# Attention backward in one kernel: TensorE sums Z and X before it transposes E, ScalarE copies E alone, and VectorE's sums move between its two products

## The chip, the cores and the metric

One Trainium2 chip, one of its cores. The metric is the time of one execution on the device in microseconds. A core has engines that run side by side, each through its own queue in order: TensorE (PE in the profile, PEld its weight loads), VectorE (DVE), ScalarE (ACT), GpSimd (POOL) and the queue that issues most DMAs (SP). They wait for each other on semaphores. SBUF is the working memory, PSUM the memory that TensorE writes to, in banks of 512 f32 a partition.

## What is computed

The reference is the forward pass and all gradients of a gated block: `out = x + attention(xn) * silu(mlp(xn))`, with `xn` a layer norm of x. Cut to the part that matters here:

```python
B, S, D, H = 1, 2048, 512, 32          # Dh = 16
qkv = (x @ wqkv) ...                   # q, k, v: 32 heads of 16
scores = einsum("bhqd,bhkd->bhqk", q, k) * Dh ** -0.5
p = softmax(scores)
o = einsum("bhqk,bhkd->bhqd", p, v)
s = o... @ wo
...
_out, _vjp = jax.vjp(_f, A_x, A_wqkv, A_wo, B_w1, B_b1, B_w2, B_b2)
_grads = _vjp(grad_out)
```

Attention and its backward pass are most of the time: for each head the 2048 x 2048 scores, their exponentials E, the products of E with the gradient of p (called G below), and sums of both over keys (for o and the gradient of q) and over queries (for the gradients of k and v).

## The kernel before

`Pre` computes the projections and the MLP's forward part; `attention_core` does attention, forward and backward together; `Grads` the rest. The change is in `attention_core` alone.

**Blocks and steps.** Heads go in 16 pairs, queries in 4 chunks of 512: 64 blocks. A block goes through 16 key tiles of 128; one tile is a step, so there are 1024 steps `g`, and 20 more at the end. The place of a step in its block is `g % 16`, 0 to 15 below. The loop at the end of `attention_core` emits one step after the other, and on each engine the instructions run in the order in which they are emitted (the order is written by hand; no scheduler moves them).

**A step on TensorE.** Before the change its order is:

- `emit_d`, `emit_s` (L1115, L1093): two matmuls d (the gradient of p, for the two heads) and two matmuls s (the scores of the *next* step), each from 32 rows of the array to 128 columns, 512 wide, so that all four run side by side.
- `emit_T(g - 1)` (L1177): seven transposes of 128 x 128 of E into one PSUM tile tT (the eighth slice of E goes by DMA).
- `emit_XT` (L1233), at place 2 alone: four f32 transposes of the sums X of the block before, into a tile XT of the pool that d uses.
- `emit_x(g - 1, ...)` (L1207, L1210, L1214): three groups of four matmuls of 128 rows to 32 (or 17) columns that add E and G into X; the third group ("g") reads the products gts of the step before.
- `emit_z(g - 20)` (L1291): four matmuls of 128 rows to 32 columns that add transposed G or E of a block 20 steps back into Z. Eight steps make one sum.

**ScalarE.** `emit_exp(g + 1)` (L1102) writes E of the next step (ets) from s; `emit_cT(g - 1)` (L1189) copies the transposed slices from tT to ek in SBUF.

**VectorE.** `emit_mult` (L1132) makes the two products gts = d x E of the two heads. Between them it copies the last `VCOPY[(g - 1) % 16]` of the seven slices of tT (0, 1 or 2 of them; ten in sixteen steps), and ScalarE's copy of the rest waits for it. Behind the products: `emit_xs` (L1223, at place 0) copies a finished X out; `emit_fin` (L1245, L1255, at place 2) copies XT to xt and makes the reciprocal rL, from which GpSimd makes the weights W1 and W2 that Z uses; `emit_acc` (L1303, L1305, at places 3 and 11) adds a finished Z to acc.

**Buffers that make engines wait.** s, tT, X and Z have one PSUM tile each: the next s waits for exp, the next transposes for the copies, the next X for xs, the next Z for acc. d and XT share three tiles: a d waits for the product that read its tile (at place 4 the first d waits for xt, the second for the first product of place 3). xs and xt share one SBUF tile.

**DMAs.** SP issues a transposing DMA of two steps' gts to gk behind every second step's products (L1148), and one or two of slices of E (ekd). GpSimd loads the next pair's operands, each load behind a small copy `tick` that waits for a product.

Of the kernel before, what the change touches and what calls it, by code (L numbers as in the profile page):

```python
# [9 lines left out]
f32 = mybir.dt.float32  # L10
# [43 lines left out]
def op_load_list(k, t, p, ld):  # L54

    L = []
    for hj in range(2):
        h = 2 * p + hj
        L.append(lambda h=h, hj=hj: ld(out=t["KVT"][32 * hj + 1:32 * hj + 17, :], in_=k.KT_s[h * 16:h * 16 + 16, :]))
        L.append(lambda h=h, hj=hj: ld(out=t["QDT"][32 * hj + 1:32 * hj + 17, :], in_=k.QT_s[h * 16:h * 16 + 16, :]))  # L60
        L.append(lambda h=h, hj=hj: ld(out=t["QDT"][32 * hj:32 * hj + 1, :], in_=k.UT_s[h:h + 1, :]))
    for hj in range(2):
        h = 2 * p + hj
        L.append(lambda h=h, hj=hj: ld(out=t["KVT"][64 + 32 * hj:80 + 32 * hj, :], in_=k.VT_s[h * 16:h * 16 + 16, :]))
        L.append(lambda h=h, hj=hj: ld(out=t["QDT"][64 + 32 * hj:80 + 32 * hj, :], in_=k.DOT_s[h * 16:h * 16 + 16, :]))
    L.append(lambda: ld(out=t["NAT"][:].rearrange("q k j c -> q k (j c)"), in_=k.NAT_s[p]))
    return L


def natq_loads(k, t, p, ld):  # L70
    return [lambda n=n, d=d: ld(out=t[n][:].rearrange("q k j c -> q k (j c)"), in_=d[p])
            for n, d in (("NATQq", k.NATQq_s), ("NATQd", k.NATQd_s))]
# [956 lines left out]
def attention_core(ctx, ctx_r, tc, k, grads, Oall, dQall, dKVT_out, ident_f32, ident_bf, npairs=16, nqc=4):  # L1029
    nc = tc.nc  # L1030
# [36 lines left out]
    st_s, st_d, st_et, st_gt, st_T = {}, {}, {}, {}, {}  # L1067
    blk = [dict(Gk={}, Ek={}) for _ in range(NB)]
    cur = {}

    def a_unit(g):
        return (g // 16, g % 16) if 0 <= g < NSTEP else None

    def z_unit(g):
        j = g // 16
        m = g % 8
        return (j, (g % 16) // 8, m % 4, m // 4) if 0 <= j < NB else None
# [38 lines left out]
                         start=True, stop=True, tile_position=(r, 0))  # L1116


    VCOPY = (0, 0, 0, 0, 1, 1, 1, 2, 1, 2, 0, 0, 1, 1, 1, 0)

    def emit_mult(g):
        a = a_unit(g)
        if a is None:
            emit_cT(g - 1, 7 - VCOPY[(g - 1) % 16], 7, nc.vector.tensor_copy)
            return
        kb = a[1]
        if kb % 2 == 0:
            cur["gts"] = gtp.tile([128, 2, 2, 512], bf16, name="gts")
        gts = cur["gts"]
        st_gt[g] = gts  # L1130
        for hj in range(2):
            nc.vector.tensor_tensor(out=gts[:, kb % 2, hj, :].rearrange("k (b q) -> k b q", b=4),  # L1132
                                    in0=st_d.pop((g, hj))[:].rearrange("k (b q) -> k b q", b=4),
                                    in1=st_et[g][:, :, hj, kb % 4, :], op=ALU.mult)
            if hj == 0:
                emit_cT(g - 1, 7 - VCOPY[(g - 1) % 16], 7, nc.vector.tensor_copy)

    def emit_dmat(g):
        a = a_unit(g)
# [28 lines left out]
    def emit_T(g):  # L1168
        a = a_unit(g)
        if a is None:  # L1170
            return
        kk = a[1] % 4
        et = st_et[g]
        t = ps_t.tile([128, 7, 128], bf16, name="tT")
        for i in range(7):
            b = i + a[1] // 4 % 2
            nc.tensor.transpose(t[:, i, :], et[:, b // 2, b % 2, kk, :], ident_bf[:])  # L1177
        st_T[g] = t
        if kk == 0:
            cur["ek"] = ekc.tile([128, 4, 7, 128], bf16, name="ek")  # L1180
            blk[a[0]]["Ek"][a[1] // 4] = cur["ek"]

    def emit_cT(g, lo, hi, copy):

        a = a_unit(g)
        if a is None or lo == hi:
            return
        j, kb = a
        copy(out=blk[j]["Ek"][kb // 4][:, kb % 4, lo:hi].rearrange("q i k -> q (i k)").bitcast(f32),  # L1189
             in_=st_T[g][:, lo:hi].rearrange("q i k -> q (i k)").bitcast(f32))  # L1190

    def emit_x(g, part):
        a = a_unit(g)
# [23 lines left out]
    def emit_xs(g):  # L1217
        a = a_unit(g)
        if a is None or a[1] != 15:
            return  # L1220
        j = a[0]
        xs = xsp.tile([128, 512], f32, name="xs", tag="xs")
        nc.vector.tensor_copy(out=xs[:], in_=blk[j].pop("X")[:])  # L1223
        blk[j]["xs"] = xs

    def emit_XT(g):
        j = g // 16 - 1
        if g % 16 != FIN_AT or not 0 <= j < NB:
            return
        xs = blk[j].pop("xs")  # L1230
        XT = ps_d.tile([128, 4, 128], f32, name="XT", tag="d")
        for qb in range(4):
            nc.tensor.transpose(XT[:, qb, :], xs[:, qb * 128:(qb + 1) * 128], ident_f32[:])  # L1233
        blk[j]["XT"] = XT
# [38 lines left out]
    def emit_z(g):  # L1273
        u = z_unit(g)
        if u is None:
            return
        j, kp, qb, part = u
        if part == 0 and qb == 0:
            blk[j]["Z"] = ps_z.tile([128, 512], f32, name="Z", tag="z")
        Z = blk[j]["Z"]  # L1280
        for par in range(2):
            kc = 2 * kp + par
            for hj in range(2):
                r = 64 * par + 32 * hj
                if part == 0:
                    mv = blk[j]["Gk"][kc][:, :, hj, qb, :]
                elif 2 * qb + hj == 7 * (1 - par):
                    mv = blk[j]["Ek"][(kc, 3)]
                else:
                    mv = blk[j]["Ek"][kc][:, :, 2 * qb + hj - par, :]  # L1290
                nc.tensor.matmul(Z[r:r + 32, :], lhsT=WT[j % 2][1 - part][:, qb, hj, :], rhs=mv,  # L1291
                                 start=(part == 0 and qb == 0), stop=(part == 1 and qb == 3), tile_position=(0, r))

    def emit_acc(g):
        u = z_unit(g)
        if u is None or u[2] != 3 or u[3] != 1:
            return
        j, kp = u[0], u[1]
        p, qc = blocks[j]
        Z = blk[j]["Z"]  # L1300
        av = acc[:, kp, :]
        if qc == 0:
            nc.vector.tensor_copy(out=av, in_=Z[:])  # L1303
        else:
            nc.vector.tensor_tensor(out=av, in0=Z[:], in1=av, op=ALU.add)  # L1305
        if qc == nqc - 1:
            ob = (outp.tile([128, 512], bf16, name="ob") if kp == 0 or j < NB - 1 else
                  xsp.tile([128, 512], bf16, name="ob", tag="xs"))
            nc.gpsimd.tensor_copy(out=ob[:], in_=av)
            dv = dKVT_out[p * 64:(p + 1) * 64, :].rearrange("r (a b s) -> r a b s", a=2, b=2)  # L1310
            for b in range(2):
                nc.gpsimd.dma_start(out=dv[:, kp, b, :], in_=ob[b * 64:(b + 1) * 64, :])

    FIN_AT = 2
    ZOFF = -20
# [4 lines left out]
    for g in range(NSTEP - ZOFF):  # L1320
        cur["g"] = g
        a = a_unit(g)
        if a is not None:
            j, kb = a
            p, qc = blocks[j]
            if kb == 0 and qc == 0:
                L = natq_loads(k, k.op0, p, nc.gpsimd.dma_start) if p > 0 else []
                if p + 1 < npairs:
                    L += op_load_list(k, OP[(p + 1) % 2], p + 1, nc.gpsimd.dma_start)
                else:  # L1330
                    L += grads.tail_loads(nc.gpsimd.dma_start)
                for i, f in enumerate(L):
                    late.append((g + 16 * (i // 4) + 6 + 3 * (i % 4), f))
        emit_d(g, 0)
        emit_s(g + 1, 0)
        emit_s(g + 1, 1)
        emit_d(g, 1)
        emit_exp(g + 1)
        emit_T(g - 1)
        emit_XT(g)  # L1340
        emit_x(g - 1, "e")
        emit_x(g - 1, "l")
        emit_x(g - 1, "g")
        emit_z(g + ZOFF)
        emit_mult(g)
        emit_xs(g - 1)
        emit_fin(g)
        for it in [x for x in late if x[0] <= g]:
            late.remove(it)

            nc.gpsimd.tensor_copy(out=tick[:], in_=st_gt[g][0:1, kb % 2, 1, 510:512])  # L1351
            it[1]()
        emit_acc(g + ZOFF)
        if g >= NSTEP:
            grads.tail_mid(g - NSTEP)
        emit_cT(g - 1, 0, 7 - VCOPY[(g - 1) % 16], nc.scalar.copy)
        st_T.pop(g - 1, None)
        emit_dmat(g)
        st_gt.pop(g - 2, None)
        st_et.pop(g - 12, None)  # L1360
        if g == NSTEP:
            ctx_r.close()
            grads.tail_open(ps_t, ps_s, ps_d)
# [113 lines left out]
```

## Time and profile before

| | us |
|---|---|
| median of the runs (3) | 2214.51 |
| lowest and highest of them | 2211.53, 2218.92 |
| the profiled execution | 2212.67 |
| its span | 2210.8 |
| attention's part of the span | 221 to 1867 |

Busy in the span: TensorE 2154.0, VectorE 1911.7, ScalarE 1734.2, GpSimd 590.4. The granted clock of TensorE is 0.997 of full speed. In the chain of work that ended last TensorE has 89%, its transposes (L1177) 24%, d 15%, X 20% in three lines, Z 10%.

How long a step of each place takes, from the start of its first d to that of the next step's, by the trace's order of time (medians over the blocks, ns):

| place | 0 | 1 | 2 | 3 | 4 | 5 | 6 | 7 | 8 | 9 | 10 | 11 | 12 | 13 | 14 | 15 |
|---|---|---|---|---|---|---|---|---|---|---|---|---|---|---|---|---|
| ns | 1562 | 1628 | 1993 | 1482 | 1670 | 1563 | 1547 | 1568 | 1554 | 1535 | 1591 | 1532 | 1635 | 1563 | 1548 | 1563 |

A line in the order of time has the start in us from the span's start, the time taken, the engine, the line, the operation and what it writes and reads, "x4" where four alike are merged, and in brackets how long the engine sat idle before and what ended that. Ends of matmuls are modelled, and their waits show best as distances between starts. A line of a group has "busy us, mean ns of one | idle before".

### The profile page before, as it was taken

What the parts mean: (1) busy time and instruction counts of PE and PEld (TensorE: products, weight loads), DVE (VectorE), ACT (ScalarE), POOL (GpSimd) and SP (SyncE); (2) the same over time, 40 slices, a digit from 0 to 9 for tenths busy, and PEclk for the clock granted to TensorE, in tenths of its full rate; (3) what the DMA queues carried; (4) which work ended last, traced back from release to release, by engine and by line L of the source; (5) the groups of instructions that cost most, each with busy time, mean ns of one, the idle gap of its engine ahead of it and who ended that gap; (6) DMA issues with size and microseconds to landing.
All of it is one profiled execution on the core that took longest, in us unless ns stands there. A gap on an engine that the chain in (4) does not pass through costs nothing.

```text
span 2210.8 us, 74213 instructions
## 1 busy us (share of the span) xinstructions
PE 2154.0 (97%) x30690; PEld 1203.2 (54%) x30690; DVE 1911.7 (86%) x3638; ACT 1734.2 (78%) x2481; POOL 590.4 (27%) x1373
## 2 busy tenths in 40 slices
PE   6999999999999999999999999999999999999998
PEld 3444555555555555555555555555555555444444
DVE  6677899999999999999999999999999998797624
ACT  4664888888888888888888888888888887784214
POOL 4375213221222222221322122222222132510002
PEclk9999999999999999999999999999999999999999
DMA  7786999999999999999999999999999999999974
GB/s 232 244 277 200 200 199 192 202 198 194 204 205 195 204 196 197 201 197 202 200 196 203 199 195 198 206 194 204 197 197 206 197 210 211 300 259 235 244 200 156
DMA packets 1422066, 461.14 MB, mean 209 GB/s; under 512 B 1334622, under 2 KB 1405918, under 8 KB 1421728
## 3 DMA queue, kind: packets, MB, share of 16 engines
q1 hardware_dynamic: 1407424, 425.46, 101.4%
q0 software_dynamic: 12720, 29.37, 5.0%
q8 instruction: 240, 3.93, 0.8%
q10 hardware_dynamic: 1584, 1.57, 0.2%
q14 instruction: 98, 0.80, 0.1%
HBM read 62.79 MB, written 64.75 MB: 58 GB/s over the span
## 4 chain that ended last, share of the span: by engine, by line
PE 89%; DVE 4%; ACT 2%; issue 2%; DMA 2%; POOL 1%; SPq 1%; ACTq 0%; DVEq 0%; POOLq 0%
PE tT L1177 24%; PE d L1115 15%; PE X L1207 10%; PE Z L1291 10%; PE X L1210 5%; PE X L1214 5%; PE s L1093 3%; PE ps_dw L742 2%; PE ps_dy L912 2%; PE ps_h L352 2%; PE ps_dw L984 2%; PE ps_m L367 2%; PE ps_dh L878 2%; PE XT L1233 1%; PE ps_qkv L210 1%
## 5 line engine op out<-in xcount | busy, mean ns | idle before, releaser
L1132 DVE TENSOR_TENSOR gts<-d,ets 128x512 bf16<-128x512 f32 x2048 | 1361.6, 683 | 99.4 <-ACT ek L1189 20.5
L1102 ACT ACTIVATE ets<-s 128x1024 bf16<-128x1024 f32 x1024 | 1047.7, 1023 | 198.6 <-PE s L1093 95.5
L1177 PE MATMUL tT<-ident_bf,ets 128*128 128x128 bf16 x7168 | 568.1, 219 | 11.7 <-ACT ek L1189 1.7
L1177 PEld LDWEIGHTS <-ets 128*128 128x128 bf16 x7168 | 444.6, 97 | 237.6 <-issue 235.5
L1189 ACT COPY ek<-tT 128x448 f32<-128x448 f32 (+2 forms) x1024 | 502.2, 490 | 2.8 <-DVE ek L1189 2.1
L1115 PE MATMUL d<-QDT,KVT 32*128 32x512 bf16 x2048 | 459.1, 385 | 0.0
L1093 PE MATMUL s<-QDT,KVT 32*128 32x512 bf16 x2048 | 401.3, 380 | 3.7 <-ACT ets L1102 3.6
L1115 PEld LDWEIGHTS <-KVT 32*128 32x128 bf16 x2048 | 145.6, 91 | 323.3 <-issue 323.3
L1207 PE MATMUL X<-ets,NAT 128*32 128x256 bf16 x4096 | 300.4, 284 | 0.3 <-DVE xs L1223 0.3
L1210 PE MATMUL X<-ets,Lc 128*32 128x256 bf16 x4096 | 289.5, 273 | 0.0
L1214 PE MATMUL X<-gts,NAT 128*17 128x256 bf16 x4096 | 289.5, 273 | 0.0
L1351 POOL COPY tick<-gts 1x2 bf16<-1x2 bf16 x205 | 35.7, 174 | 612.3 <-DVE gts L1132 612.3
L1291 PE MATMUL Z<-gk,W 128*32 128x512 bf16 x2048 | 197.9, 379 | 1.0 <-DVE acc L1305 1.0
L1291 PE MATMUL Z<-ek,W 128*32 128x512 bf16 x1792 | 198.4, 379 | 0.0
L1207 PEld LDWEIGHTS <-NAT 128*32 128x32 bf16 x4096 | 106.0, 93 | 110.8 <-issue 11.3
L1256 POOL TENSOR_TENSOR W<-NATQq,rL 128x128 bf16<-128x128 bf16 x64 | 25.4, 396 | 526.1 <-DVE rL L1255 438.4
L1093 PEld LDWEIGHTS <-KVT 32*128 32x128 bf16 x2048 | 139.2, 91 | 12.8 <-issue 9.6
L1189 DVE COPY ek<-tT 128x64 f32<-128x64 f32 (+1 forms) x576 | 131.6, 229 | 0.7
L1291 PEld LDWEIGHTS <-W 128*32 128x32 bf16 x4096 | 109.8, 97 | 11.5 <-issue 1.5
L1210 PEld LDWEIGHTS <-Lc 128*32 128x32 bf16 x4096 | 107.8, 96 | 0.0
L1214 PEld LDWEIGHTS <-NAT 128*17 128x17 bf16 x4096 | 103.4, 92 | 3.0
L1291 PE MATMUL Z<-ekd,W 128*32 128x512 bf16 x256 | 97.0, 379 | 0.0
(246 smaller groups left out, 2318.7 us busy)
## 6 DMA issues: line engine op xcount, KB each, us to landing
gk<-gts SPq DMA_TRANSPOSE x512, 5.3
H1T_s<-h1r SPq DMA_DIRECT2D x28, 256.0 KB, 4.1
HGT_s<-hgT SPq DMA_DIRECT2D x8, 896.0 KB, 4.5
DH_s<-stg SPq DMA_DIRECT2D x12, 512.0 KB, 3.2
hch<-DH_s SPq DMA_DIRECT2D x12, 512.0 KB, 4.4
gp<-H1T_s SPq DMA_DIRECT2D x9, 512.0 KB, 7.6
out_dram<-ob_w POOLq DMA_DIRECT2D x36, 128.0 KB, 4.2
NAT_s<-NS SPq DMA_DIRECT2D x4, 1056.0 KB, 6.1
```

Source lines behind the costliest of these rows:

```text
L352: nc.tensor.matmul(ps[:], lhsT=w1_sb[:, ic, fc * 128:(fc + 1) * 128], rhs=yT[:, ic, g * 512:(g + 1) * 512], start=(ic == 0), stop=(ic == I ...
L367: nc.tensor.matmul(ps[:], lhsT=hgT[:, g % 2, fc, t4 * 128:(t4 + 1) * 128], rhs=w2_sb[:, fc, :], start=(fc == 0), stop=(fc == FC - 1))
L1093: nc.tensor.matmul(s[:, hj, :], lhsT=op["KVT"][r:r + 32, kb * 128:(kb + 1) * 128], rhs=op["QDT"][r:r + 32, qc * 512:(qc + 1) * 512], start ...
L1102: nc.scalar.activation(out=st_et[g][:, :, :, a[1] % 4, :].rearrange("k b h q -> k h b q"), in_=cur["s"][:].rearrange("k h (b q) -> k h b q ...
L1115: nc.tensor.matmul(d[:], lhsT=op["KVT"][r:r + 32, kb * 128:(kb + 1) * 128], rhs=op["QDT"][r:r + 32, qc * 512:(qc + 1) * 512], start=True, ...
L1132: nc.vector.tensor_tensor(out=gts[:, kb % 2, hj, :].rearrange("k (b q) -> k b q", b=4), in0=st_d.pop((g, hj))[:].rearrange("k (b q) -> k b ...
L1177: nc.tensor.transpose(t[:, i, :], et[:, b // 2, b % 2, kk, :], ident_bf[:])
L1189: copy(out=blk[j]["Ek"][kb // 4][:, kb % 4, lo:hi].rearrange("q i k -> q (i k)").bitcast(f32), in_=st_T[g][:, lo:hi].rearrange("q i k -> q ...
L1207: nc.tensor.matmul(X[r:r + 32, 0:256], lhsT=NATt[:, kb, hj, 1:33], rhs=ev, start=(kb == 0), stop=False, skip_group_check=True, tile_positi ...
L1210: nc.tensor.matmul(X[r:r + 32, 256:512], lhsT=Lc[:], rhs=ev, start=False, stop=False, skip_group_check=True, tile_position=(0, r))
L1214: nc.tensor.matmul(X[r:r + 17, 256:512], lhsT=NATt[:, kb, hj, 0:17], rhs=gv, start=False, stop=(kb == 15), skip_group_check=True, tile_pos ...
L1291: nc.tensor.matmul(Z[r:r + 32, :], lhsT=WT[j % 2][1 - part][:, qb, hj, :], rhs=mv, start=(part == 0 and qb == 0), stop=(part == 1 and qb = ...
```

## The change

In the step on TensorE, Z goes to the front, behind d and s; X follows; the transposes T and, at place 2, XT come last. ScalarE copies all seven slices of tT; VectorE copies none. On VectorE xs and acc move from behind the second product to between the two products; at the places where there is no product they stand alone. xt and rL stay behind the second product. DMAs, buffers and sizes stay as they are.

```diff
-    VCOPY = (0, 0, 0, 0, 1, 1, 1, 2, 1, 2, 0, 0, 1, 1, 1, 0)
...
     def emit_mult(g):
         a = a_unit(g)
         if a is None:
-            emit_cT(g - 1, 7 - VCOPY[(g - 1) % 16], 7, nc.vector.tensor_copy)
+            emit_xs(g - 1)
+            emit_acc(g + ZOFF)
             return
...
             if hj == 0:
-                emit_cT(g - 1, 7 - VCOPY[(g - 1) % 16], 7, nc.vector.tensor_copy)
+                emit_xs(g - 1)
+                emit_acc(g + ZOFF)
...
-        copy(out=blk[j]["Ek"][kb // 4][:, kb % 4, lo:hi].rearrange("q i k -> q (i k)").bitcast(f32),
-             in_=st_T[g][:, lo:hi].rearrange("q i k -> q (i k)").bitcast(f32))
+        nc.scalar.copy(out=blk[j]["Ek"][kb // 4][:, kb % 4].rearrange("q i k -> q (i k)").bitcast(f32),
+                       in_=st_T[g][:].rearrange("q i k -> q (i k)").bitcast(f32))
...
         emit_exp(g + 1)
-        emit_T(g - 1)
-        emit_XT(g)
+        emit_z(g + ZOFF)
         emit_x(g - 1, "e")
         emit_x(g - 1, "l")
         emit_x(g - 1, "g")
-        emit_z(g + ZOFF)
+        emit_T(g - 1)
+        emit_XT(g)
         emit_mult(g)
-        emit_xs(g - 1)
         emit_fin(g)
...
-        emit_acc(g + ZOFF)
         if g >= NSTEP:
             grads.tail_mid(g - NSTEP)
-        emit_cT(g - 1, 0, 7 - VCOPY[(g - 1) % 16], nc.scalar.copy)
+        emit_cT(g - 1)
```

More of the change, by code (lines that the diff above doesn't have):

```diff
@@ L1181, in emit_T, with emit_cT @@
             blk[a[0]]["Ek"][a[1] // 4] = cur["ek"]
-    def emit_cT(g, lo, hi, copy):
+    def emit_cT(g):
         a = a_unit(g)
-        if a is None or lo == hi:
+        if a is None:
             return
         j, kb = a
-        copy(out=blk[j]["Ek"][kb // 4][:, kb % 4, lo:hi].rearrange("q i k -> q (i k)").bitcast(f32),
-             in_=st_T[g][:, lo:hi].rearrange("q i k -> q (i k)").bitcast(f32))
+        nc.scalar.copy(out=blk[j]["Ek"][kb // 4][:, kb % 4].rearrange("q i k -> q (i k)").bitcast(f32),
+                       in_=st_T[g][:].rearrange("q i k -> q (i k)").bitcast(f32))
     def emit_x(g, part):
```

## The prediction

> **What bounds the kernel now.** I read the busy times by stage first, then the longest waits, then the order of time within single steps; a share of busy time says little where the same pattern of 1.6 us repeats 1024 times.
>
> ```profile
> 221.00:1867.00 1646.00, 1630.57 (x27804) 950.36 (x27801) 1543.62 (x2941) 1445.04 (x2048) 405.85 (x1136) 1.00 1.16 200
> ...
> ACT ets L1102 <- PE s L1093: 95.5, 535, 0.5
> ...
> L1189 ACT COPY ek<-tT 128x448 f32<-128x448 f32 (+2 forms) x1024 | 502.2, 490 | 2.8 <-DVE ek L1189 2.1
> ...
> L1189 DVE COPY ek<-tT 128x64 f32<-128x64 f32 (+1 forms) x576 | 131.6, 229 | 0.7
> ```
>
> The change lies in one stretch, 221 to 1867 us, 1646 us of 2210.8, or 1.61 us for each of 1024 steps. TensorE (PE, 1630.57 busy), VectorE (DVE, 1543.62) and ScalarE (ACT, 1445.04) are all nearly full, so the step's loops of waits decide. Here is a plain step, of place 14 in its block:
>
> ```profile
> 1016.65 0.39 PE L1093 MATMUL s<-QDT,KVT 32*128 32x512 bf16 x2
> ...
> 1017.02 0.55 PE L1177 MATMUL tT<-ident_bf,ets 128*128 128x128 bf16 x7
> ...
> 1017.14 1.02 ACT L1102 ACTIVATE ets<-s 128x1024 bf16<-128x1024 f32 x1 [0.17 <-PE s L1093]
> ...
> 1017.84 0.39 PE L1291 MATMUL Z<-gk,W 128*32 128x512 bf16 x4
> ...
> 1018.06 0.47 ACT L1189 COPY ek<-tT 128x384 f32<-128x384 f32 x1
> ...
> 1018.22 0.39 PE L1093 MATMUL s<-QDT,KVT 32*128 32x512 bf16 x2
> ...
> 1018.70 1.02 ACT L1102 ACTIVATE ets<-s 128x1024 bf16<-128x1024 f32 x1 [0.17 <-PE s L1093]
> ```
>
> Loop one, scores and exp: s at 1016.65, exp 0.49 later at 1017.14, its end at 1018.16, next s 0.06 after that. s has one buffer, so no step can be shorter than 0.49+1.02+0.05 = 1.56 us. Loop two, transposes: T waits for the copies of the T before (one buffer, too): 0.05 after the copy ends. From T to the next T but one that is 1.14 (T, X, Z, d) + 0.52 (exp) + 0.92 + copy + 0.05: 3.16 with a full copy of 0.53, or 1.58 a step; VectorE's slices shorten it to 1.555 and 1.53. So two loops stand almost level. TensorE alone needs less: the one step in each block that waits for neither (place 3) takes 1.48.
>
> The rest is in the special places, 2 to 4 here:
>
> ```profile
> 1023.33 0.55 PE L1177 MATMUL tT<-ident_bf,ets 128*128 128x128 bf16 x7
> ...
> 1023.72 0.61 PE L1233 MATMUL XT<-ident_f,xs 128*128 128x128 f32 x4
> ...
> 1024.59 0.39 PE L1291 MATMUL Z<-ek,W 128*32 128x512 bf16 x4
> ...
> 1024.60 0.68 DVE L1245 COPY xt<-XT 128x512 f32<-128x512 f32 x1
> ...
> 1024.91 0.39 PE L1115 MATMUL d<-QDT,KVT 32*128 32x512 bf16 x1
> ...
> 1025.43 1.25 DVE L1132 TENSOR_TENSOR gts<-d,ets 128x512 bf16<-128x512 f32 x2
> ...
> 1026.39 0.38 PE L1115 MATMUL d<-QDT,KVT 32*128 32x512 bf16 x1
> ...
> 1026.61 0.68 DVE L1305 TENSOR_TENSOR acc<-Z,acc 128x512 f32<-128x512 f32 x1
> ...
> 1027.74 0.39 PE L1291 MATMUL Z<-gk,W 128*32 128x512 bf16 x4
> ```
>
> At place 2 XT runs half way through the step and is done long before xt copies it (1024.60, right behind the products). Then products, then acc, which ends at 1027.29, well before Z wants its bank at 1027.74. By the starts of d, the medians of the 16 places add up to 25.53 us; 16 x 1.561 would be 24.98, so 0.55 a block is lost here (XT 0.44 of TensorE's time). The mean block is 25.72: 0.18 more in scattered stalls, which I leave as they are.
>
> **The change, part by part**, in places of a block and then times 64 blocks.
>
> *VectorE's copies go.* 131.6 us of VectorE, 576 copies, are removed. ScalarE's copy is 0.527 for all seven slices and 0.054 less for each slice taken away; ten slices in sixteen steps come back: 0.54 a block, 35 us of ScalarE. They lie in its idle time (198.6 us before exp) if the next exp still starts on time; that is the next point.
>
> *T last in the step.* From s: d and s take 0.32, then Z 0.22, X 0.23 to its third group, 0.21 to T, 0.33 to T's last: 1.32. The copy can start 0.26 after that, seen once at the end of the stretch, where the copy waited for T:
>
> ```profile
> 1867.32 0.55 PE L1177 MATMUL tT<-ident_bf,ets 128*128 128x128 bf16 x7 [0.25 <-ACT ek L1189]
> ...
> 1867.91 0.53 ACT L1189 COPY ek<-tT 128x448 f32<-128x448 f32 x1 [0.64 <-PE tT L1177]
> ...
> 1869.34 0.66 PE L1233 MATMUL XT<-ident_f,xs 128*128 128x128 f32 x4
> ...
> 1870.03 0.69 DVE L1245 COPY xt<-XT 128x512 f32<-128x512 f32 x1 [0.91 <-PE XT L1233]
> ```
>
> The copy's line starts 0.04 after T's line ends. So it starts 1.58 after s, and the next exp 0.43 later (0.53 less the 0.10 by which exp and copy overlap: 1018.06 is 0.92 after 1017.14, not 1.02), at 2.01. Loop one wants it at 1.56+0.48 = 2.04. It fits by 0.03: cost nothing, covered by loop one, and loop two is gone, since T now comes 0.5 after the copy it waits for. Bounds: with 0.31 from T to the copy (ScalarE behind o_tp at L577) the exps come late and it is +0.08 a block; without the overlap +0.35. I take the rows of the same instructions, 0.26 and 0.10.
>
> *TensorE's changes of tile shape.* Every change of shape in the trace costs 0.094 to 0.10 over streaming (Z to d 0.31 against 0.22 between full matmuls of 512; T to X 0.149 against 0.055; X to d 0.205 against 0.109; d to T 0.32). The step had three and keeps three, but d to Z, 32 rows to 32 columns, never occurs. I take 0.32. Without any charge for it a block would be 0.17 shorter; at 0.36, the median from d to T with its waits, 0.10 longer. The Trainium skill, TensorEngine Tiling (Array Packing), section Key Properties, says that changing the tiling mode drains TensorE, which speaks against the uncharged value; by its rule the switch stays at about 0.10 and the sum as it is. The four kinds that the trace has agree, at 0.094 to 0.10.
>
> *xs between the products, place 0.* X is done 0.87 into the step, xs starts 0.40 later (1.27), the second product 0.60 after that, done at 2.55. The next step's third X group wants it at 1.56+0.87 = 2.43 and gets it at 2.60: 0.17 of stall, 0.09 of it in TensorE's slack (1.56 less 1.47). Net +0.07. (xs no longer delays place 1's products from behind, but nothing waited there.)
>
> *XT last, place 2.* XT's fourth starts at 0.99+0.33+0.06+0.33 = 1.71, next d 0.20 later: the step is 1.91, +0.35 over 1.56; before, it cost about the same (1.99 with its T waiting). But xt now waits for XT: 1.71+0.31 = 2.02. xt and rL take 0.83, so place 3's first product starts at 2.85, 0.94 into its step instead of 0.53.
>
> *acc between the products, place 3.* Queued on VectorE: product 0.94, acc 1.54 to 2.22, second product 2.14 to 2.82. Place 3 itself is short, 1.47. At place 4 Z comes first and needs acc out of its bank: wanted 0.45, got 2.22+0.05-1.47 = 0.80. X's third group then would start at 1.25 and waits for the second product: 2.82+0.05-1.47 = 1.40. T at 1.61, next d at 2.09. Against 1.56 and the 0.12 that s was already late, s comes +0.41 late at place 5. Two exps behind late copies add 0.03 and 0.04. At place 11, the other acc, VectorE is on time: Z's bank is free at 0.25 of place 12 against 0.42, and the product at 0.85 against 0.87: nothing, though with 0.02 to spare.
>
> *Other queues.* The transposing DMAs on SP keep their order, are released by the second product, at most about 1 us later at places 0 to 4, and Z reads them 14 steps on; POOL's W after rL ends about 3.4 us after the start of place 2, Z needs it at 4.2. Nothing.
>
> *Sum.* A block: 24.98 + 0.07 + 0.35 + 0.03 + 0.41 + 0.04 = 25.88, against 25.53: +0.35, times 64 = +22 us. The profiled execution took 2212.67 (span 2210.8 and 1.9 around it), so 2235; the median of the runs shown, 2214.51, is 1.8 higher. I say 2236. The forecast's own range, from the bounds above one or two at a time (25.69 to 26.26): 2223 to 2260.
>
> **The rivals.** *ScalarE's loop takes over, slower still.* If the copy starts more than about 0.30 after T's last, or exp cannot overlap it, every step grows: up to 0.035 a step, another 22 us, 2240 to 2265. For it: only 0.03 of slack, and one row of the wait. Against: that row is the same instruction.
>
> *The tail behind XT stays hidden.* If VectorE has acc and the second product done before place 4 asks, 0.27 a block goes, 25.61: +5 us, 2218, and with fewer scattered stalls as low as 2208. It decides at the second product of place 3 ending 0.6 us earlier than I reckon. Against: its order and durations are fixed.
>
> *VectorE sets the step now, faster.* It is busy 1543.62 of 1646, the most of those whose busy time is not modelled. Its block is 32 products at 0.60, two acc and xs at 0.60, xt and rL 0.83, the copies 1.31: 23.1 us, and 21.8 without copies; were it the pace, the block would fall by up to 1.31, stopped by loop one at 24.98: at most 47 us, 2166 to 2200. Against: in 9 of 16 places the first product starts 0.48 to 0.49 after d, so VectorE waits for TensorE. The Trainium skill, Perfetto Trace Analysis, section Identifying the Most-Contended Engine, says to take occupancy for VectorE and ScalarE and to optimize the engine with the highest; this is that rule's case for the change, and the starts of the products are what this trace has against it.
>
> **How the numbers follow.** Forecast 0.60; ScalarE's loop 0.15; hidden tail 0.13, which lies within 0.3% (6.6 us, about what a measurement of this kernel can tell); VectorE as pace 0.08; 0.04 for a gain that I don't see (scattered stalls, 12 us in all, going). Slower 0.75, same 0.13, faster 0.12. The range 2206 to 2262 leaves out the fast case and the upper part of ScalarE's.
>
> **What would show it.** Right: plain steps still 1.56 with s 0.05 after exp; T never waiting for a copy; place 4 about 2.1 long, its Z released by acc and its last X group by the second product; xt waiting for XT about 0.25 in each block; place 1 about 1.7. Wrong: plain steps of 1.58 or more with exp released by the copy; plain steps under 1.55; place 4 at 1.6; d to Z far from 0.32.

## The result, and the profile after

The changed kernel takes 2226.93 us (median of 13 runs, 2223.39 to 2248.1), the kernel before, run beside it, 2211.53 us (median of 13 runs, 2208.65 to 2218.92). The ratio is 1.0071, 95% interval 1.0051 to 1.0090: slower by 0.7%, or 15.4 us. The forecast was +22 us. The longest run, 2248.1, had a granted clock of 0.946, the other twelve 0.996 to 0.998. The profiled execution of the changed kernel took 2224.65 us, with a span of 2222.8; attention went from 1644.4 to 1660.6 us in it (first d to last), +16.2, and the stage ahead of attention happened to be 3.1 us shorter.

From the page of the profiled execution before: the chain that ended last, exp, and a group of Z.

```profile
PE 89%; DVE 4%; ACT 2%; issue 2%; DMA 2%; POOL 1%; SPq 1%; ACTq 0%; DVEq 0%; POOLq 0%
...
L1102 ACT ACTIVATE ets<-s 128x1024 bf16<-128x1024 f32 x1024 | 1047.7, 1023 | 198.6 <-PE s L1093 95.5
...
L1291 PE MATMUL Z<-gk,W 128*32 128x512 bf16 x2048 | 197.9, 379 | 1.0 <-DVE acc L1305 1.0
```

From the page after: the busy times, the chain that ended last, and three groups (busy us, mean ns of one | idle before them and what ended most of it).

```profile
PE 2162.1 (97%) x30639; PEld 1197.3 (54%) x30690; DVE 1833.9 (83%) x3062; ACT 1804.7 (81%) x2481; POOL 592.3 (27%) x1373
...
PE 84%; DVE 8%; ACT 2%; issue 2%; DMA 2%; SPq 1%; POOL 1%; DVEq 0%; ACTq 0%; POOLq 0%
...
L1102 ACT ACTIVATE ets<-s 128x1024 bf16<-128x1024 f32 x1024 | 1049.8, 1025 | 28.7 <-PE s L1093 19.2
L1188 ACT COPY ek<-tT 128x448 f32<-128x448 f32 x1024 | 545.5, 533 | 118.5 <-PE tT L1177 55.2
...
L1290 PE MATMUL Z<-gk,W 128*32 128x512 bf16 x2048 | 203.6, 389 | 15.1 <-DVE acc L1304 11.4
```

VectorE became 78 us less busy (1911.7 before), and yet its share of the chain doubled, from 4% to 8%. Less work and more of the end: that is work in a worse place. ScalarE's idle time moved from in front of exp (198.6 before, 28.7 now) to in front of the copy (2.8 before, 118.5 now): it is the copy that waits for TensorE now, as it must with T last. This group of Z lost 15.1 us in waits, mostly for acc; before, it lost 1.0.

Three new ones among the longest waits of attention (what waited <- for what: us in total, times, longest us):

```profile
ACT ek L1188 <- PE tT L1177: 53.6, 140, 0.9
...
DVE xt L1244 <- PE XT L1232: 16.3, 61, 0.5
...
PE Z L1290 <- DVE acc L1304: 10.0, 44, 0.2
```

xt waits for XT in nearly every block, 0.27 us each time. Before, xt waited for XT only once, for the last block's sums, behind the end of the stretch (the row at 1870.03 that the prediction shows).

A plain step of the changed kernel in the order of time (start, time taken, engine, line, operation; place 8 of a block, and the start of place 9):

```profile
1036.72 0.39 PE L1093 MATMUL s<-QDT,KVT 32*128 32x512 bf16 x2
...
1037.19 1.02 ACT L1102 ACTIVATE ets<-s 128x1024 bf16<-128x1024 f32 x1
...
1037.70 0.56 PE L1177 MATMUL tT<-ident_bf,ets 128*128 128x128 bf16 x7
...
1038.27 0.39 PE L1093 MATMUL s<-QDT,KVT 32*128 32x512 bf16 x2
1038.28 0.38 PE L1115 MATMUL d<-QDT,KVT 32*128 32x512 bf16 x1
1038.30 0.53 ACT L1188 COPY ek<-tT 128x448 f32<-128x448 f32 x1
1038.59 0.40 PE L1290 MATMUL Z<-ek,W 128*32 128x512 bf16 x4
...
1038.74 1.02 ACT L1102 ACTIVATE ets<-s 128x1024 bf16<-128x1024 f32 x1
```

From s to s it takes 1.55 us: exp 0.47 after s, 1.02 long, the next s 0.06 after its end. The copy starts behind T and the next exp comes right behind the copy, 0.44 after its start. From d to the first Z, the change of tile shape that the trace of before did not have, it is 0.31.

Places 2 to 4 of the same block, where the time went:

```profile
1027.90 0.61 PE L1232 MATMUL XT<-ident_f,xs 128*128 128x128 f32 x4
...
1028.54 0.69 DVE L1244 COPY xt<-XT 128x512 f32<-128x512 f32 x1 [0.27 <-PE XT L1232]
...
1029.39 0.65 DVE L1131 TENSOR_TENSOR gts<-d,ets 128x512 bf16<-128x512 f32 x1
...
1029.92 0.38 PE L1115 MATMUL d<-QDT,KVT 32*128 32x512 bf16 x1
1029.95 0.68 DVE L1304 TENSOR_TENSOR acc<-Z,acc 128x512 f32<-128x512 f32 x1
...
1030.55 3.23 DVE L1131 TENSOR_TENSOR gts<-d,ets 128x512 bf16<-128x512 f32 x5
1030.69 0.40 PE L1290 MATMUL Z<-gk,W 128*32 128x512 bf16 x4 [0.23 <-DVE acc L1304]
...
1031.12 0.45 PE L1213 MATMUL X<-gts,NAT 128*17 128x256 bf16 x4
1031.50 0.56 PE L1177 MATMUL tT<-ident_bf,ets 128*128 128x128 bf16 x7
...
1032.00 0.39 PE L1115 MATMUL d<-QDT,KVT 32*128 32x512 bf16 x1
```

Read it as one queue, VectorE's. XT is last in place 2, so xt waits for it and starts at 1028.54. rL, the first product of place 3 (1029.39), acc (1029.95) and the second product (the first of the five merged at 1030.55) follow without a gap. TensorE, meanwhile, is through place 3 and starts place 4 with d at 1029.92; its Z starts 0.77 later, when acc is done. Its third X group begins at 1031.12 with the matmul that needs the first product alone; the next one waits once more, for the second product. The step lasts 2.08 us.

Medians of the step's length by place (from first d to first d) in ns, of the kernel before, the kernel after, and the first experiment below:

| place | 0 | 1 | 2 | 3 | 4 | 5 | 6 | 7 | 8 | 9 | 10 | 11 | 12 | 13 | 14 | 15 | sum |
|---|---|---|---|---|---|---|---|---|---|---|---|---|---|---|---|---|---|
| before | 1562 | 1628 | 1993 | 1482 | 1670 | 1563 | 1547 | 1568 | 1554 | 1535 | 1591 | 1532 | 1635 | 1563 | 1548 | 1563 | 25534 |
| after | 1551 | 1693 | 1925 | 1482 | 2083 | 1481 | 1613 | 1552 | 1551 | 1551 | 1550 | 1550 | 1594 | 1509 | 1586 | 1552 | 25823 |
| XT ahead of T | 1551 | 1692 | 1962 | 1481 | 1690 | 1482 | 1613 | 1551 | 1550 | 1553 | 1550 | 1550 | 1593 | 1510 | 1584 | 1552 | 25464 |

The block grew by 0.29 us by medians and by 0.25 by means (25.72 to 25.97); 64 blocks at 0.25 are the 16 us of attention. Place 4 alone grew by 0.41; all the others together gave 0.12 back.

### The profile page after: what moved, and what is told of

The parts are those of the page before. It is cut to its first block, busy times and chain, and to the rows that moved or that the text cites. A ratio compares the mean times of both kernels' runs of the same rounds, so it can differ in the third digit from the quotient of the medians.

```text
span 2222.8 us, 73754 instructions
## 1 busy us (share of the span) xinstructions
PE 2162.1 (97%) x30639; PEld 1197.3 (54%) x30690; DVE 1833.9 (83%) x3062; ACT 1804.7 (81%) x2481; POOL 592.3 (27%) x1373
## 3 DMA queue, kind: packets, MB, share of 16 engines
q10 hardware_dynamic: 1584, 1.57, 0.2%
## 4 chain that ended last, share of the span: by engine, by line
PE 84%; DVE 8%; ACT 2%; issue 2%; DMA 2%; SPq 1%; POOL 1%; DVEq 0%; ACTq 0%; POOLq 0%
PE tT L1177 21%; PE Z L1290 14%; PE d L1115 13%; PE X L1213 6%; PE X L1206 5%; PE X L1209 5%; PE s L1093 3%; PE ps_dy L912 2%; PE ps_dw L984 2%; PE ps_h L352 2%; PE ps_m L367 2%; PE ps_dh L878 2%; DVE gts L1131 2%; DVE xt L1244 2%; PE XT L1232 1%
## 5 line engine op out<-in xcount | busy, mean ns | idle before, releaser
L1131 DVE TENSOR_TENSOR gts<-d,ets 128x512 bf16<-128x512 f32 x2048 | 1315.4, 684 | 176.9 <-PE d L1115 64.1
L1102 ACT ACTIVATE ets<-s 128x1024 bf16<-128x1024 f32 x1024 | 1049.8, 1025 | 28.7 <-PE s L1093 19.2
L1188 ACT COPY ek<-tT 128x448 f32<-128x448 f32 x1024 | 545.5, 533 | 118.5 <-PE tT L1177 55.2
L1177 PE MATMUL tT<-ident_bf,ets 128*128 128x128 bf16 x7168 | 579.0, 221 | 0.0
L1177 PEld LDWEIGHTS <-ets 128*128 128x128 bf16 x7168 | 403.6, 98 | 205.8 <-issue 184.5
L1115 PE MATMUL d<-QDT,KVT 32*128 32x512 bf16 x2048 | 480.5, 385 | 0.0
L1213 PE MATMUL X<-gts,NAT 128*17 128x256 bf16 x4096 | 312.4, 273 | 0.2
L1206 PE MATMUL X<-ets,NAT 128*32 128x256 bf16 x4096 | 290.9, 273 | 0.0
L1115 PEld LDWEIGHTS <-KVT 32*128 32x128 bf16 x2048 | 160.0, 90 | 110.4 <-issue 11.0
L1290 PE MATMUL Z<-gk,W 128*32 128x512 bf16 x2048 | 203.6, 389 | 15.1 <-DVE acc L1304 11.4
L1093 PEld LDWEIGHTS <-KVT 32*128 32x128 bf16 x2048 | 154.2, 90 | 17.0 <-issue 10.0
L1213 PEld LDWEIGHTS <-NAT 128*17 128x17 bf16 x4096 | 119.4, 91 | 26.0 <-issue 21.1
L1304 DVE TENSOR_TENSOR acc<-Z,acc 128x512 f32<-128x512 f32 x96 | 65.4, 681 | 2.9 <-PE Z L1290 2.9
```

Of the source, the lines that this page charges most:

```text
L1093: nc.tensor.matmul(s[:, hj, :], lhsT=op["KVT"][r:r + 32, kb * 128:(kb + 1) * 128], rhs=op["QDT"][r:r + 32, qc * 512:(qc + 1) * 512], start ...
L1102: nc.scalar.activation(out=st_et[g][:, :, :, a[1] % 4, :].rearrange("k b h q -> k h b q"), in_=cur["s"][:].rearrange("k h (b q) -> k h b q ...
L1115: nc.tensor.matmul(d[:], lhsT=op["KVT"][r:r + 32, kb * 128:(kb + 1) * 128], rhs=op["QDT"][r:r + 32, qc * 512:(qc + 1) * 512], start=True, ...
L1188: nc.scalar.copy(out=blk[j]["Ek"][kb // 4][:, kb % 4].rearrange("q i k -> q (i k)").bitcast(f32), in_=st_T[g][:].rearrange("q i k -> q (i ...
L1206: nc.tensor.matmul(X[r:r + 32, 0:256], lhsT=NATt[:, kb, hj, 1:33], rhs=ev, start=(kb == 0), stop=False, skip_group_check=True, tile_positi ...
L1213: nc.tensor.matmul(X[r:r + 17, 256:512], lhsT=NATt[:, kb, hj, 0:17], rhs=gv, start=False, stop=(kb == 15), skip_group_check=True, tile_pos ...
```

## The experiments

The theory: the loss is one queue on VectorE, xt held by XT, then product, acc, product, which TensorE meets at place 4. The rivals: that ScalarE's longer copy makes the loss, or that T last lengthens every step through the copy, or that the changed order is worse by itself through the new change of tile shape. Each ratio below is against the kernel before on the same chip; its median there is 2211.81 or 2211.07, beside 2211.53 above, so times of different experiments can be set side by side to about 1 us.

### XT ahead of T, the rest as changed

```diff
-        emit_T(g - 1)
         emit_XT(g)
+        emit_T(g - 1)
```

> The changed kernel with one swap: XT ahead of T at place 2, all else as changed. Theory (VectorE's queue behind XT holds Z and X at place 4): XT's fourth starts 0.39 earlier, xt starts right behind the second product (1.68 into place 2 instead of 2.06) and waits for nothing, place 4 falls from 2.08 to about 1.78, a block by 0.33 us: 21 us less than the changed kernel, about 2206, level with or 0.2% below the kernel before. Rival (ScalarE alone with the copies is what costs): T comes 0.39 later at place 2 and its copy with it, so no gain, or a few us more than 2227.

Measured: 2204.62 us, ratio 0.9961 [0.9949, 0.9973]. Two lines exchanged turn the loss of 0.7% into a gain of 0.4%. Places 2 to 4 of the same block in this kernel's order of time:

```profile
1016.48 0.66 PE L1232 MATMUL XT<-ident_f,xs 128*128 128x128 f32 x4
1016.97 0.55 PE L1177 MATMUL tT<-ident_bf,ets 128*128 128x128 bf16 x7
1017.18 0.68 DVE L1244 COPY xt<-XT 128x512 f32<-128x512 f32 x1
...
1018.02 0.65 DVE L1131 TENSOR_TENSOR gts<-d,ets 128x512 bf16<-128x512 f32 x1
...
1018.58 0.68 DVE L1304 TENSOR_TENSOR acc<-Z,acc 128x512 f32<-128x512 f32 x1
...
1018.94 0.39 PE L1115 MATMUL d<-QDT,KVT 32*128 32x512 bf16 x1
...
1019.40 0.40 PE L1290 MATMUL Z<-gk,W 128*32 128x512 bf16 x4
...
1020.63 0.39 PE L1115 MATMUL d<-QDT,KVT 32*128 32x512 bf16 x1
```

xt has no wait in its brackets any more: it runs straight behind the second product of place 2. acc ends at 1019.26, and Z starts 0.46 after the place's first d instead of 0.77. Place 4 is 1.690, 0.39 shorter, and the table's other places are as they were, but place 2, 0.04 longer. So the queue behind XT is the cause of the loss, and nothing else in the change is needed to explain it. The plain steps with ScalarE's full copies, T last and the new change of shape are in this kernel too, and it is the faster one.

### acc moved to another place, XT left last

Z's sums one step later, so that acc falls to places 4 and 12, away from the queue behind XT:

```diff
-    ZOFF = -20
+    ZOFF = -21
```

> The changed kernel with Z 21 steps back instead of 20, so that acc falls on places 4 and 12 instead of 3 and 11; XT stays last. Theory: xt still comes late (2.06 into place 2), but acc no longer stands between it and the second product of place 3; Z at place 4 waits for nothing, place 4 falls from 2.08 to about 1.66, place 5 grows from 1.48 to about 1.65 (its last X group behind acc and the second product): 0.36 us less a block, 23 us less than the changed kernel, about 2204. Rival (ScalarE alone): nothing that ScalarE does moves, so 2227.

Measured: 2207.15 us, ratio 0.9980 [0.9970, 0.9990]. Place 4 is 1.630 and place 5 1.646, 3.276 together against 3.564 after and 3.172 with XT ahead. XT is still last and xt still waits for it, as long as after:

```profile
DVE xt L1244 <- PE XT L1232: 16.3, 61, 0.5
```

So the wait of xt costs nothing by itself: places 2 to 5 together take 6.682 here and 6.687 in the last kernel below, where XT is ahead and acc at place 4 as well. It costs when acc stands behind it. The queue's two halves are shown apart by these kernels.

By medians this block is as short as that with XT ahead (25.451 against 25.464), but the mean block of the profiled execution is 0.27 above its medians (there 0.16). Part of that can be seen in the waits of this kernel:

```profile
ACT ets L1102 <- DMA ekd<-ets: 8.6, 8, 2.5
```

Eight times exp waited for the DMA that reads an older E out of its buffer, 8.6 us in all; after, it was three times and 2.1 us. This profiled execution took 2214.01 us, the longest of the kernel's 12, so the median run probably has less of it.

### ScalarE alone in the order of before

```diff
-    VCOPY = (0, 0, 0, 0, 1, 1, 1, 2, 1, 2, 0, 0, 1, 1, 1, 0)
+    VCOPY = (0, 0, 0, 0, 0, 0, 0, 0, 0, 0, 0, 0, 0, 0, 0, 0)
```

> The kernel before with one part of the change alone: ScalarE copies all seven slices, VectorE none; the order on TensorE and of VectorE's sums as before. Theory: loop two (T behind the copy of the T before) is then 1.58 in all steps instead of in six of sixteen, the places with VectorE's slices (5 to 10, 12 to 15) grow by about 0.015 to 0.03: 0.13 to 0.2 us a block, 8 to 13 us, 2220 to 2225. Rival (ScalarE alone is the whole loss): 15 us and more, 2227 or above. If VectorE's slices had been a burden on VectorE, this would be faster than before.

Measured: 2214.18 us, ratio 1.0013 [1.0005, 1.0022]; some 2 to 3 us, where 8 to 13 were expected. Two plain steps of it, in the order of time:

```profile
1031.70 1.02 ACT L1102 ACTIVATE ets<-s 128x1024 bf16<-128x1024 f32 x1
...
1032.62 0.53 ACT L1189 COPY ek<-tT 128x448 f32<-128x448 f32 x1
...
1033.19 0.55 PE L1177 MATMUL tT<-ident_bf,ets 128*128 128x128 bf16 x7
...
1033.30 1.02 ACT L1102 ACTIVATE ets<-s 128x1024 bf16<-128x1024 f32 x1
...
1034.22 0.53 ACT L1189 COPY ek<-tT 128x448 f32<-128x448 f32 x1
...
1034.79 0.55 PE L1177 MATMUL tT<-ident_bf,ets 128*128 128x128 bf16 x7
```

This is loop two as the prediction described it: each T starts 0.04 after the copy of the T before, with a full copy every time. The steps alternate, 1.598 and 1.555, or 1.577 on average where the prediction had 1.58. The block is 0.12 longer by medians, the 8 us expected, but only 0.07 by means (25.79 against 25.72), since fewer scattered stalls fell on it. (The kernel before has VectorE's slices at nine places, 5 to 10 and 13 to 15, not ten; seven steps in sixteen had the full copy already.) That ScalarE's work as such makes the loss is out: it costs about 3 us here, 1 to 5 by the interval, of 15.4.

### VectorE's slices kept in the changed order

The changed kernel with the table VCOPY of before, its slices between the products, ScalarE's copy of the rest behind them.

```diff
...
             if hj == 0:
+                emit_cT(g - 1, 7 - VCOPY[(g - 1) % 16], 7, nc.vector.tensor_copy)
                 emit_xs(g - 1)
...
-        emit_cT(g - 1)
+        emit_cT(g - 1, 0, 7 - VCOPY[(g - 1) % 16], nc.scalar.copy)
```

> The changed kernel with VectorE's slices of T kept between its products, as before; TensorE's new order, and ScalarE copying the rest. Theory: T ends at the end of the step now, so the slice's copy waits for it on VectorE and the second product stands behind that copy; X's last group in the next step waits for the product: places 5 to 10 and 13 to 15 grow from 1.55 to about 1.68 to 1.75, 1.4 us a block, 90 us more than the changed kernel, about 2318. Rival (ScalarE's longer copies are the loss): ScalarE is relieved by 35 us, and the time falls to about 2212.

Measured: 2326.95 us, ratio 1.0527 [1.0510, 1.0543]. A place with two slices, in the order of time:

```profile
1088.56 0.56 PE L1181 MATMUL tT<-ident_bf,ets 128*128 128x128 bf16 x7
...
1089.16 0.29 DVE L1193 COPY ek<-tT 128x128 f32<-128x128 f32 x1 [0.27 <-PE tT L1181]
...
1089.36 1.28 DVE L1134 TENSOR_TENSOR gts<-d,ets 128x512 bf16<-128x512 f32 x2
1089.48 0.42 ACT L1193 COPY ek<-tT 128x320 f32<-128x320 f32 x1 [0.35 <-DVE ek L1193]
...
1089.80 1.03 ACT L1102 ACTIVATE ets<-s 128x1024 bf16<-128x1024 f32 x1
...
1089.94 0.44 PE L1218 MATMUL X<-gts,NAT 128*17 128x256 bf16 x4
```

With T last, the slice comes when T is done, and both engines stand behind it: VectorE's product, which X waits for, and ScalarE's copy, which exp waits for; which of the two sets the step was not separated. The steps that follow one with slices (places 6 to 11, 14, 15 and 0, one later than expected) take 1.69 to 1.76. So ScalarE's copies belong to T last: by themselves they cost about 3 us, and left out of the new order they cost 100 (2326.95 less 2226.93).

### The sums behind the products, in the changed order

```diff
...
             if hj == 0:
-                emit_xs(g - 1)
-                emit_acc(g + ZOFF)
...
         emit_mult(g)
+        emit_xs(g - 1)
```

and acc behind the loads, as before.

> The changed kernel with xs and acc back behind the second product; TensorE's order and ScalarE's copies as changed. Theory: with Z first in the step, acc behind the product ends 0.5 to 0.6 too late for Z at places 4 and 12 (about 2.54 and 1.99 instead of 2.08 and 1.59), and xs too late for X at place 1 (1.78): 0.9 us more a block, 58 us more than the changed kernel, about 2285. Rival (the sums between the products are the loss, because the second product comes late): this undoes it, and the time falls to about 2212.

Measured: 2289.11 us, ratio 1.0351 [1.0335, 1.0367]. Places 3 and 4 in the order of time:

```profile
1061.52 0.38 PE L1115 MATMUL d<-QDT,KVT 32*128 32x512 bf16 x1
...
1062.15 0.68 DVE L1299 TENSOR_TENSOR acc<-Z,acc 128x512 f32<-128x512 f32 x1
...
1062.89 0.40 PE L1285 MATMUL Z<-gk,W 128*32 128x512 bf16 x4 [0.82 <-DVE acc L1299]
...
1064.05 0.38 PE L1115 MATMUL d<-QDT,KVT 32*128 32x512 bf16 x1
```

Z waits for acc behind both products; place 4 is 2.52, place 12 2.04 (after: 2.08 and 1.59), and place 1, behind xs, 1.92 (1.69). Z first needs its sums taken out early: the move between the products is worth 62 us there.

### The sums between the products, in the order of before

The counterpart, this part of the change alone, with Z last and VectorE's slices.

```diff
...
             if hj == 0:
+                emit_xs(g - 1)
+                emit_acc(g + ZOFF)
...
-        emit_xs(g - 1)
...
-        emit_acc(g + ZOFF)
```

> The kernel before with one part of the change alone: xs and acc between the products; TensorE's order and VectorE's slices as before. Theory: with Z last in the step Z's sum ends only at the end of the step, so acc waits for Z on VectorE and the second product stands behind it: at places 4 and 12 X's last group waits for that product, at place 1 too: 0.62 to 0.69 us a block, 40 to 44 us, about 2253. Rival (the place of the sums on VectorE matters little by itself): within 5 us of the kernel before.

Measured: 2263.01 us, ratio 1.0234 [1.0219, 1.0249], 52 us slower where 40 to 44 were reckoned. Places 4 and 12 are 1.903 each (before 1.670 and 1.635), place 2 2.064 (1.993). By medians the block is 0.73 longer, which is 47 us; scattered stalls make up the rest. The waits of attention in this kernel show the mechanism:

```profile
DVE acc L1309 <- PE Z L1295: 37.8, 88, 0.6
...
DVE acc L1307 <- PE Z L1295: 13.0, 30, 0.6
```

With Z last in the step, acc between the products comes before the Z that it adds is done: VectorE stands 0.43 us each time, with the second product behind it, and X wants that product. Neither wait was there before. xs waits for its X in the same way, 13.8 us in 60 blocks. The same move is worth 62 us with Z first and costs 52 us with Z last.

### X last where its products come late

XT ahead of T, as in the first experiment, and at places 1 and 4 T ahead of X, so that the late product has more time:

```diff
-        emit_x(g - 1, "e")
...
+        if g % 16 not in (1, 4):
+            emit_x(g - 1, "e")
...
         emit_XT(g)
         emit_T(g - 1)
+        if g % 16 in (1, 4):
+            emit_x(g - 1, "e")
...
```

The lines left out are the same for the other two groups of X, and XT's old place.

> The changed kernel with XT ahead of T, and at places 1 and 4 alone X behind T, so that X's last group asks later for the second product that xs or acc held up. Theory: place 1 falls from 1.69 to about 1.65, place 4 (with XT ahead, 1.69) stays near 1.7 as Z still waits there, X's waits go at both: 0.13 us less a block than with XT ahead alone, 8 us, about 2197, 0.65% below the kernel before. If X's wait at these two places is not what is left, no gain over XT ahead alone (2205).

Measured: 2204.32 us, ratio 0.9971 [0.9962, 0.9981]: no gain over XT ahead alone. Place 1 fell from 1.692 to 1.666 only, and place 4 rose from 1.690 to 1.727. With XT ahead, place 4's T already came 0.29 after the start of X's third group, against 0.21 in a plain step, so 0.08 at most was to be had there; the expectation had taken more of the step for a wait than was in it.

### XT ahead, X last at place 1, Z one step later

The first, the second and half of the last experiment together.

> The changed kernel with XT ahead of T, X behind T at place 1, and Z 21 steps back (acc at places 4 and 12). Theory: the three waits on VectorE (xt for XT, acc in front of place 3's second product, xs in front of place 0's) are each taken off the path; a block 0.18 us shorter than with XT ahead alone, 11 us, about 2194, 0.8% below the kernel before; what is left over 1.55 a step is XT itself (0.35). If the gains are the same wait counted twice, it stays at 2203 to 2205.

Measured: 2202.28 us, ratio 0.9968 [0.9955, 0.9980]; the gain over XT ahead alone that was expected is not there. By medians of its steps the block is 25.430, 0.034 less than 25.464, or 2 us in 64 blocks; the medians of the runs differ by 2.3 us and the ratios not at all. The repairs do not add up: X last at place 1 brings that place from 1.692 to 1.665, as in the experiment before, but once the queue behind XT is out of place 4, moving acc as well wins nothing more.

XT ahead (2204.62), with or without these additions, beats both kernels; Z one step later with XT left last (2207.15) does so too, by less.

## Why the prediction was right, point by point

- **Direction and place: right.** The term that made the forecast slower was place 4, +0.41 a block, by VectorE's queue behind XT. It was forecast 2.09 long with Z at 0.80 and T at 1.61; the medians are 2.083, 0.771 and 1.585. Putting XT ahead removes 0.39 of it, and with it the loss: this is shown, not only argued. The rival that the tail behind XT stays hidden is out: place 3's second product ends 1.32 into place 4, forecast 1.35.
- **XT last, place 2: right.** Forecast 1.91, measured 1.925; xt at 2.02 from the step's start, measured 2.03; waiting "about 0.25", measured 0.27.
- **xs between the products, place 0: right.** Place 1 was forecast about 1.70, and is 1.693, by X's third group waiting for the second product.
- **The new change of tile shape: right.** d to Z takes 0.314, forecast 0.32; between full Z and X it is 0.216, so 0.098 is the charge. The Trainium skill, TensorEngine Tiling (Array Packing), section Key Properties, states that a change of tiling mode drains TensorE. The 0.098 us agrees with it for this kind too; a drain as such cannot be seen in the trace.
- **VectorE's copies and T last: right in outcome, off in the sum.** Plain steps were costed at 1.56, with exp 0.49 after s. They are 1.551: exp starts 0.470 after the second s (0.476 after the first) in every plain step, against 0.482 in most steps of before, where ScalarE stood idle ahead of exp. 0.476 + 1.025 + 0.05 is 1.551, so loop one still sets the step; the prediction had named anything under 1.55 as a sign of being wrong. Sixteen steps at 0.01 are 0.16 a block, or 10 us of the forecast that did not come. The size of the copies was a little off as well: the table VCOPY adds up to eleven slices in sixteen steps, not ten, and ScalarE's copies grew by 43 us (502.2 to 545.5), not 35, still without cost to the step.
- **"It fits by 0.03": the slack was smaller, and enough.** Exp follows the copy's start by 0.442 in plain steps and by 0.429 at least (places 2, 5 and 13, where s was done early), so 0.013 is left. The rival that ScalarE's loop takes over did not happen, but it was near.
- **Place 12, "nothing, though with 0.02 to spare": it was 0.04 late.** The second product of place 11 ends 0.83 into place 12, and 0.05 later releases X's third group, which wanted it at 0.84: 0.04 a block, 3 us, lost.
- **The sum: close, and in part by luck.** Forecast 25.88 a block, measured 25.82 by medians: +0.29 instead of +0.35, 18 us instead of 22. Two errors of opposite sign stand behind that: plain steps of 1.551 instead of 1.561 make the block 0.16 shorter, and the special places together are 1.01 over sixteen plain steps instead of 0.90, of which place 12 is 0.04. By means it is +0.25, since 0.15 of scattered stalls came in place of 0.19. The forecast of the time, 2236, stood on the three runs' median of 2214.51, 3.0 above that of thirteen; that is a third of the 9 us by which it was too high.
- **VectorE as the pace: refuted.** With 78 us less of VectorE's busy time, and the loss at place 4 removed as well, the kernel gained 0.4%, not up to 47 us. The Trainium skill, Perfetto Trace Analysis, section Identifying the Most-Contended Engine, chooses the engine to optimize by occupancy, which pointed at VectorE here. What held the step was a loop through s and exp, and what held place 4 was an order on VectorE, not an amount of work.

## What to carry to other kernels

Ask of each moved instruction who queues behind it on the engine that consumes it: here four transposes that came 0.6 us later in their step held a copy that nobody waited for, and through the product and acc queued behind it a PSUM bank that TensorE waited for. Parts of a reordering can have opposite signs alone and together (sums between the products: -62 us with Z first, +52 us with Z last), so try them in the order they are meant for. And when a reordering loses a little, look for the one place that lost a lot before undoing it: fifteen of sixteen places were together faster here, and exchanging two lines made the change a gain.

## What the runs showed of the hardware

- exp starts 0.470 us after the second s in the changed kernel's plain steps, 0.480 to 0.482 in most steps of the kernel before, and 0.506 in every second step of the kernel with ScalarE alone in the old order; these few values recur to within some ns. Where ScalarE came straight from a copy it was mostly 0.470, but it was so in other steps too, and what chooses between the values stays open.
- Two instructions of ScalarE back to back overlap in the records: the exp starts 0.43 to 0.44 after the start of a copy that takes 0.53, the copy 0.92 after the start of an exp that takes 1.02.
- Scattered stalls (mean block, the first included, less the sum of the medians) cost 0.04 to 0.28 us a block in the profiled executions and differ between kernels that are alike step by step. Some are exp waiting for the DMA that reads E (10.9 us of attention in the worst case seen, the kernel before with the sums between the products); what delays that DMA was not tried, and the rest has no cause named here.
